# A gated linear attention and a feed-forward layer: scores by halves of 64 keys in two more units, with a new order of all work

## The chip, the cores and the metric

The kernel runs on one core of a Trainium2 chip. Its time is the time of one execution on the device in microseconds; the figure of a kernel is the median over runs. Three runs of the kernel before gave 575.72, 575.88 and 578.43, median 575.88 us.

## What is computed

For each of 4 batches and 8 heads, a state of 48 x 48 complex numbers is decayed by a complex factor per key row and step, and takes in the outer product of key and value; the output is the query times the real part of the state. The result goes through a feed-forward layer with the gate h * tanh(softplus(h)).

```python
mag = np.sqrt(a_re * a_re + a_im * a_im)
scale = np.minimum(mag, 0.999) / (mag + 1e-06)
a_re_n, a_im_n = a_re * scale, a_im * scale
for t in range(S):                        # S = 768, D = 48
    new_re = ar * S_re - ai * S_im        # ar, ai: step t of a_re_n, a_im_n
    new_im = ar * S_im + ai * S_re
    S_re, S_im = new_re + outer(k[t], v[t]), new_im
    y[t] = q[t] @ S_re
h = x @ w_in                              # x: y with heads side by side, 3072 x 384; w_in 384 x 2048
out = (h * np.tanh(softplus(h))) @ w_out  # w_out 2048 x 384
```

## The kernel before, in words

The 3072 tokens are cut into 12 units of 256 (three for each batch), a unit into two chunks a and b of 128 tokens. For a unit, `elementwise` turns decay factors into growth and angle per step, scales queries and keys by them and sends the result through DMAs ("relay": tiles X and QK into T, six for a chunk) into a layout with the 96 rows of one head below each other.

`attention` then does, for each chunk: transposes of the keys (`kn`, tile pkn), the scores keys x queries in two groups of four heads (`am`, tile pa), their masking by VectorE (`am_out`, tiles am or kept), the weighted sums of the values plus the old state times the queries (`y`, tile ypsum), and the new state (`pd`, `add`). The output moves by DMA (`x move`) into the input of the feed-forward layer `moe`. There each unit from 1 on has eight pairs p0 to p7 of 256 columns of the hidden layer. A pair has first-layer matmuls (`mm1`, tile ph, line 787), the gate (exp, square, ln and inv on ScalarE, cap and gate on VectorE, tile e and g), the split into a high and a low half (gh, gl) and second-layer matmuls (`mm2`, tile po, line 824). Unit 0 does it in blocks q0 to q3 for each chunk, without a split. The weights arrive as 64-bit words; VectorE and ScalarE turn them into floats in the first part of the run.

Scores exist in two forms, chosen by the unit's number against `HALF`. In one piece (line 637), a head is one matmul of 128 keys by 128 queries, and the mask is one VectorE instruction of 128 x 512 (line 652). By halves (line 644), the first 64 keys go with all 128 queries and the last 64 keys with the last 64 queries only, two heads side by side in the two column halves of the array. The mask is then three instructions (line 659, into one of two kept tiles whose unused corners are zeroed once), and the odd heads' weighted sums read values whose halves are swapped (`Vs`, loaded beside V).

No engine's order is left to a scheduler: each operation has a number by its place in the program text, and the table `ORDER` lists them as they are issued. A letter behind a number puts the operation on another engine than its first choice (V VectorE, A ScalarE, G GpSimd, T TensorE, S SyncE). Each engine works through its own part of that list in order, and SyncE's part is the queue of its DMAs: a DMA whose data isn't there yet holds all behind it. Eighty matmuls on a constant ("spins", line 886) fill TensorE at the start.

Of the kernel before, what the change touches and what calls it, by code (L numbers as in the profile page):

```python
# [25 lines left out]
DM, DF = H * D, 2048  # L26
P = 128
# [5 lines left out]
NCH = TU // C  # L33
# [13 lines left out]
HALF = 3  # L47
# [8 lines left out]
72 0 1 73 127 3 74 2 75 128 7V 5 8 76 10V 4 9 11 77 6 12 192 78 13 202 197 14 79 24V 80 27V 81 82 25 83 169V 15 19 28  # L56
26 132V 84 16 166V 85 133 22 17 86 167 23 87 31 170 88 32 135V 18 134 34 33 29 137 89 21 136 90 20 91 42 47 46G 45 92
35 48 30 49 93 43 36 44 194 50 193 53 52 94 139 39 95 54 195 96 55 97 40 51 98 37 196V 99 38 100 56A 60 207 101 62A
140 562 102 204 57 563 103 203V 104 199 105 41 200 106 61A 138 107 58 64 108 142 109 59 205 112 66 116 67A 68 113 118
65A 117 70 71A 114 206V 123 69 198 110 119 217 141 120 124 115V 121 201V 125 430 63 143 209 212 126 567 208V 210 144  # L60
122 146 186 211V 145 130 168 153 570V 147A 185 173 171 149 148 568 184 151 111 218V 187 174 155 154 571G 360A 129 175
150V 160 152 156 222 157 432 219 569 158 220 356 163 573 161 164 214 159 221V 273 172 189 357 215 188 213 272 191 162
176 216V 361A 190 358 177 359 227 274 165 363 178 575 275 365 367 276 364 223 224 282 366 572 181A 368 277 225 283 369
576 232 182 179 370 226V 278 292 131 180 229 237 284 279 293 376A 371 183 230 280 374 228 578 574 281 285 231V 372
375A 286 303 378 242 373 287 233V 386 234 388 362 583 302 235 387 382 389 390 288 236V 294 392 434 289 247 383 295 304
312 584 296 385 238 239 379 290 391 381A 384 393 297 380 291 240 442 743 305 243 395 377 244 577 241V 394 298 245 252
306 397 744 400 307 246V 398 446 299 401 257 248 579 322 396 399 308 402 249 403 448 405 580 313 749 404 250 406 323
314 581 251V 407 582 315 262 309 409 316 564 585 408 594A 317 565 300 593 586 324 253 254 301 436 410 431 318 411 263
255 412 258 325 264 414 326 256V 415 587A 417 265 450 267 418 413 332 266V 327 421 259 440 420 433 310 328 566 588 452
423 333 422 438 319 260 343 334 329 589 335 320 592 321 590 428V 595 435 336 311 591 596 426 424 330 337 429 597 603  # L70
342 602 598 338 331 425 344 604 427 268 269 601 339 463 750 747 345 609 270 346 462 607 752 474 261V 475 340 347 271V
341 606 751 416 437 348 476 349 350 351 599 605 444 612 608 477 464 419 456 478 610 454 439 753 757 487 354 613 600
441 755 465 479 352 466 355 611V 758 443 616 617 467 445 614 754G 615 621 619 353 480 618 623 468 759 622 481 486 469
760 447 756 498 488 761 624 458 499 765 470 500 489 490 628 936 511 471 762 472 626 944 501 473 625 491 620 629 627
449 745 631 492 764 630 510 493 451 502 935 941 482A 632 635 522 633 634 766 503 512 504 523 483 484 494A 746 636 453
513 505 455 942 495 485 496 497 514 524 525 515 767 506 763 459 516 526 517 507 768A 527 639 534 769 518 774 535 528
792 775A 529 508 509 641 776A 536 547 537 519 546 771 778 772 781 530A 520 531 642 779 773 637 638 780 640 785 787 788
521 532 533 644 786 791 538 643 539 548 549 540 541 793 655 457 943 460 946 656 550 542A 543 544 461 545 551 782 945G
645 646 777 552 770 553 947 948 783 957 554 668 796 958 797V 794 959 667 748 555 784 798 960 647 648 795 649 650 1127
799 961 949 657 658 950 669 800 556 651A 557 801 670 790 679 558 802 652 805 1133V 962 659 803 952 560 660 671 1128  # L80
661 807 808 806 662 653 940 951 680 953 804 789 809 672 810V 1134 954 811 692 681 682 812 815 816 813 1136 814 663A
1135 691 818 673 559 683 956 939 938 1138 674 820 955 664 684 965V 817 822 819V 654 665 666 937 967 693 561 685 694
704 968A 686 703 715 675A 676 677 826 964 678 969A 971 966 1137 974 1140 825 828 978 827 695 984 716 696 697 698 982
687A 688 728 963 1141 970 1149 705 706 689 699A 1150 700 823 707 708 981 690 701 702 821 717 727 718 1151 709 1139 979
# [12 lines left out]
1045 1513 1036 1046 1064 1053 1357 1047A 1054 1198 931V 1063 1514 1522 1055 1056 1356 1075 1065 1347 1057 933V 1199
1355 1048 1515 1066 1352 1200 1523 1037 1038 1049 1524 932 1343 1203 1204 1516 1058 1059 934 1076 1067 1201 1068 1069
1050 1077 1070 1087 1078 1079 1080 1081 1060 1517 1088 1518 1089 1520 1090 1061 1202 1082 1091 1205V 1519 1207 1092
1093 1071 1502 1099 1206 1100 1101 1062 1532A 1525 1526 1072 1529V 1102 1103 1208 1112 1360 1361 1111 1358 1359 1349  # L100
1083 1084 1094 1095 1113 1073 1362 1364 1363 1501 1365 1691 1114 1074 1210 1531 1697 1209 1104 1105 1366 1106 1371
1096 1369 1372 1700V 1115 1370 1116 1117 1698 1367 1085 1701 1222 1699 1702 1528 1118 1533G 1373 1535 1536 1368 1704
1086 1537 1530 1542 1534 1221 1211 1212 1223 1224 1107 1374 1527 1097 1098 1375 1108 1376V 1119A 1233 1213 1120 1538
1214 1703 1215 1225 1226 1234 1109 1216 1217 1873 1705 1227 1110 1121 1122 1123 1257 1228 1379 1229 1377 1706 1218
1235 1236 1237 1544 1380 1124 1541 1378 1230 1713 1238 1714 1715 1239 1240 1241 1874 1546 1258 1543 1245 1125 1126
1539 1246 1707 1247 1248 1545 1547 1386 1249 1250 1381 1382 1387 1384 1270 1540 1259 1260 1383V 1391 1390 1251 1252
1261 1262 1263 1219 1220 1231 1232 1879 1880 1716 1242 1264 1269 1385 1708 1709 1293 1253 1265 1271 1272 1710 1389
1281 1254 1504 1882 1881 1884 1273 1274 1275 1395 1396 1392 1397 1398 1276 1393 1294 1295 1243 1296 1244 1394 1883G
# [105 lines left out]
def tile_kernel(ctx, tc, q, k, v, vs, are, aim, are_t, aim_t, w_in, w_out, out):  # L214
# [900 lines left out]
```

## Time and profile before

| what | before |
|---|---|
| median of three runs | 575.88 us |
| the profiled execution, its own time | 579.47 us |
| its span, first to last instruction | 577.7 us |
| TensorE matmul busy | 567.0 us (98%) |
| VectorE busy | 482.4 us (83%) |
| ScalarE busy | 471.8 us (82%) |
| granted clock of TensorE | 0.998 |

The span is what the trace covers; the rest of the execution lies around it. An engine's busy share is an average over the run; how full it is in a stretch is a matter of the slices and of the table by stretches.

### The profile page before, as it was taken

To read this page: it belongs to the slowest core of one execution; us is meant where nothing else is said; L and a number is where in the kernel's file an instruction comes from. 1 tells how busy PE (TensorE), PEld (TensorE's weight loads), DVE (VectorE), ACT (ScalarE), POOL (GpSimd) and SP (SyncE) were. 2 spreads that over 40 slices of the span, in tenths; PEclk is the share of its full clock that TensorE was granted. 3 is DMA by queue.
4 is the path that set the end of the run, shared out by engine and by line. 5 is a ranking of instruction groups with operands and counts; after the bars stand their busy time and mean duration, and the time that the engine had idled before them with its cause. 6 is when DMAs were issued, how large, how long until landed. Compare 5 with 4: busy or idle time off the path is not lost.

```text
span 577.7 us, 13275 instructions
## 1 busy us (share of the span) xinstructions
PE 567.0 (98%) x5262; PEld 532.3 (92%) x5262; DVE 482.4 (83%) x899; ACT 471.8 (82%) x759; POOL 29.5 (5%) x59
## 2 busy tenths in 40 slices
PE   8999999999999999999999999999999999999996
PEld 4689788899999999999999999999999999999995
DVE  5999999999999999989979997998876867556453
ACT  7899999999999999888977688868967868456671
POOL 2010000110000010200002000300000000000000
PEclk9999999999999999999999999999999999999999
DMA  8688874521626345262244145072253260010100
GB/s 297 235 275 267 251 237 131 168 58 38 196 77 177 108 128 159 60 188 61 65 135 146 23 133 163 19 211 75 59 145 101 65 170 1 15 44 0 56 2 33
DMA packets 58469, 68.91 MB, mean 119 GB/s; under 512 B 4976, under 2 KB 51440, under 8 KB 58400
## 3 DMA queue, kind: packets, MB, share of 16 engines
q1 hardware_dynamic: 57616, 67.14, 39.5%
q8 instruction: 43, 0.70, 0.5%
q10 hardware_dynamic: 720, 0.66, 0.4%
q14 instruction: 26, 0.21, 0.1%
q0 software_dynamic: 64, 0.20, 0.1%
HBM read 39.52 MB, written 4.72 MB: 77 GB/s over the span
## 4 chain that ended last, share of the span: by engine, by line
PE 74%; ACT 12%; DVE 7%; DMA 3%; issue 2%; POOL 1%; SPq 0%; ACTq 0%; DVEq 0%; POOLq 0%
PE ph L787 30%; PE po L824 29%; PE ypsum L674 6%; PE pa L644 4%; ACT X L174 3%; PE pd L689 3%; ACT L172 2%; ACT e L174 2%; PE pkn L622 2%; DMA words<-w_out 1%; DMA words<-w_in 1%; DMA T<-QK 1%; ACT words L174 1%; ACT R L174 1%; DVE w L296 1%
## 5 line engine op out<-in xcount | busy, mean ns | idle before, releaser
L174 ACT ACTIVATE e<-e 128x512 f32<-128x512 f32 x192 | 119.1, 629 | 27.6 <-DVE e L856 25.4
L787 PE MATMUL ph<-xH,wh 128*128 128x256 f32 x462 | 133.3, 289 | 0.0
L787 PE MATMUL ph<-xL,wh 128*128 128x256 f32 x462 | 129.9, 281 | 0.0
L787 PE MATMUL ph<-xH,wl 128*128 128x256 f32 x462 | 129.8, 281 | 0.0
L824 PE MATMUL po<-wh,gh 128*128 128x384 f32 x308 | 105.0, 341 | 0.0
L824 PE MATMUL po<-wh,gl 128*128 128x384 f32 x308 | 103.5, 336 | 0.4 <-DVE gl L812 0.4
L824 PE MATMUL po<-wl,gh 128*128 128x384 f32 x308 | 103.6, 336 | 0.0
L787 PEld LDWEIGHTS ph<-xH,wh 128*128 128x128 f32 x462 | 87.0, 188 | 1.8 <-issue 0.7
L787 PEld LDWEIGHTS ph<-xL,wh 128*128 128x128 f32 x462 | 87.0, 188 | 0.3 <-DVE xL L758 0.3
L787 PEld LDWEIGHTS ph<-xH,wl 128*128 128x128 f32 x462 | 87.0, 188 | 0.0
L800 DVE SCALAR_TENSOR_TENSOR g<-e,ph 128x512 f32<-128x512 f32 x96 | 65.1, 682 | 22.9 <-ACT e L174 19.8
L174 ACT ACTIVATE e<-ph 128x512 f32<-128x512 f32 x96 | 56.6, 592 | 26.4 <-PE ph L787 21.9
L812 DVE TENSOR_TENSOR gl<-g,gh 128x512 fp32r<-128x512 f32 x88 | 63.7, 725 | 10.1 <-PE po L824 8.7
L174 ACT ACTIVATE e<-e,fifth 128x512 f32<-128x512 f32 x96 | 69.4, 723 | 1.9
L824 PEld LDWEIGHTS po<-wh,gl 128*128 128x128 f32 x308 | 57.9, 188 | 0.7 <-DVE gl L812 0.7
L824 PEld LDWEIGHTS po<-wh,gh 128*128 128x128 f32 x308 | 57.9, 188 | 0.6 <-issue 0.2
L824 PEld LDWEIGHTS po<-wl,gh 128*128 128x128 f32 x308 | 57.9, 188 | 0.0
L856 DVE TENSOR_SCALAR e<-e 128x512 f32<-128x512 f32 x96 | 42.5, 445 | 17.8 <-ACT e L174 17.5
L172 ACT ACT_TABLE_LOAD x36 | 46.2, 1283 | 0.6
L659 DVE TENSOR_TENSOR kept<-pa,cmask 64x128 f32<-64x128 f32 (+1 forms) x108 | 32.6, 329 | 13.4 <-PE pa L644 10.6
L674 PE MATMUL ypsum<-T,S 96*48 96x128 f32 x320 | 34.3, 275 | 0.0
L174 ACT ACTIVATE X<-X 128x768 f32<-128x768 f32 (+1 forms) x40 | 30.2, 764 | 0.2
(145 smaller groups left out, 1116.5 us busy)
## 6 DMA issues: line engine op xcount, KB each, us to landing
T<-QK SPq DMA_DIRECT2D x70, 129.0 KB, 2.8
T<-X SPq DMA_DIRECT2D x69, 129.0 KB, 2.6
words<-w_in SPq DMA_DIRECT2D x8, 768.0 KB, 6.4
words<-w_out SPq DMA_DIRECT2D x8, 768.0 KB, 6.5
QK<-k SPq DMA_DIRECT2D x12, 384.0 KB, 5.4
QK<-q SPq DMA_DIRECT2D x12, 384.0 KB, 5.6
V<-v SPq DMA_DIRECT2D x12, 384.0 KB, 4.3
R<-a_re SPq DMA_DIRECT2D x12, 384.0 KB, 4.2
```

Source lines behind the costliest of these rows:

```text
L172: self.nc.scalar.preload_act_table_set(need)
L174: return self.nc.scalar.activation(out, in_, func, **kw)
L622: e.transpose(d["pkn", g][:, i, :], T()[:, 4 * g + i, 1, :C], ident)
L644: e.matmul(d["pa", g][r0:r0 + C // 2, i, k0:], T()[:, 4 * g + i, 1, k0:k0 + C // 2], T()[:, 4 * g + i, 0, k0:C], start=True, stop=True)
L659: e.tensor_tensor(x[r, :, two, t], y[r, :, two, t], m[r, :, two, t], ALU.mult)
L674: e.matmul(ypsum[64 * par:64 * par + D, i, :], lhs, rhs, start=m == 0, stop=first or m == 1)
L689: e.matmul(d["pd", g][r, i, :], d["kn"][:, h, r], st["V"][:, c, h * D:(h + 1) * D], start=not held, stop=not held or i == 3)
L787: e.matmul(ph[k][:, slot(k, j, a), :], win(x, j, kt, a), st[y][:, kt, cols(k)], start=n == 0, stop=n + 1 == len(todo))
L800: e.scalar_tensor_tensor(g_[k], e_[k], 2.5, ph[k], ALU.subtract, ALU.mult)
L812: e.tensor_tensor(gs[k][1], g_[k], gs[k][0].bitcast(F32), ALU.subtract)
L824: e.matmul(po[t], x[:, slot(k, j, a), 0 if halved else t * P:C if halved else (t + 1) * P], wout(y, j, a), start=j == 0 and a == 0 and n == 0,
L856: op("V", f"{n} cap", lambda e, k=k: e.tensor_scalar_min(e_[k], e_[k], math.exp(20.0)))
```

## The change

`HALF` goes from 3 to 1: units 1 and 2 have their scores by halves as well, and take `Vs` from a tile of their own with one buffer. The table `ORDER` is another one, with two more entries (the two loads of Vs). The numbers of the operations shift with these, so a line of it is not to be read against the other table.

```diff
-HALF = 3
+HALF = 1
...
-72 0 1 73 127 3 74 2 75 128 7V 5 8 76 10V 4 9 11 77 6 12 192 78 13 202 197 14 79 24V 80 27V 81 82 25 83 169V 15 19 28
+0 7V 8 1 9 10V 12 3 11 2 13 24V 72 73 14 128 25 15 27V 136V 26 74 16 127 170V 75 76 167V 77 78 79 80 81 82 83 168 19
...
+    EARLY = (1, 2)
...
         if u >= HALF:
-            st.homes["Vs"] = lambda: swapped["Vs"][:, u % 2]
+            if u in EARLY:
+                st.homes["Vs"] = io, "Vs", 1, [P, NCH, DM // 2]
+            else:
+                st.homes["Vs"] = lambda: swapped["Vs"][:, u % 2]
             op("S", f"Vs{u} load", lambda e: e.dma_start(st["Vs"], vs[u]))
```

Between the two programs, the matmuls of scores change from 48 + 144 + 144 (whole, first half, second half) to 16 + 176 + 176. On VectorE 12 masks in one piece and 108 of the halves become 4 and 132, and the two zero fills come from GpSimd. ScalarE has 40 table loads where it had 36. SyncE issues all 144 relays, where ScalarE issued five.

VectorE around the masks of unit 1's first chunk, in the order before (line 652 is the mask in one piece, 292, 296 and 300 are steps of the weights, 856 is the cap of a gate):

```order
L800 SCALAR_TENSOR_TENSOR g<-e,ph 128x512
L856 TENSOR_SCALAR e<-e 128x512
L515 SCALAR_TENSOR_TENSOR X_464<-rmask,I 128x384
L292 TENSOR_SCALAR w<-words 128x768
L652 TENSOR_TENSOR am<-pa,cmask 128x512 x2
L296 SCALAR_TENSOR_TENSOR w<-words,w 128x768
L856 TENSOR_SCALAR e<-e 128x512
```

The same place now (the lines behind 336 have moved by one, those behind 403 by four: 663 is the masks of the halves, 738 a zero fill, 860 the cap):

```order
L804 SCALAR_TENSOR_TENSOR g<-e,ph 128x512
L738 MEMSET kept 128x512
L292 TENSOR_SCALAR w<-words 128x768
L663 TENSOR_TENSOR kept<-pa,cmask 128x4x64
L663 TENSOR_TENSOR kept<-pa,cmask 64x2x64 x2
L296 SCALAR_TENSOR_TENSOR w<-words,w 128x768
L860 TENSOR_SCALAR e<-e 128x512
L515 SCALAR_TENSOR_TENSOR I<-ncar,I 128x3
L663 TENSOR_TENSOR kept<-pa,cmask 128x4x64
L663 TENSOR_TENSOR kept<-pa,cmask 64x2x64 x2
```

Two instructions have become six, with a zero fill ahead of them and two other steps between the groups.

TensorE at the first chunk of unit 2, before: its last state matmuls (pd), and what follows, three steps of nine first-layer matmuls (ph), the first three of the 27 rows shown:

```order
L689 MATMUL pd<-V,kn 64x48
L689 MATMUL pd<-V,kn 33x48
L787 MATMUL ph<-xH,wh 128x256
L787 MATMUL ph<-xL,wh 128x256
L787 MATMUL ph<-xH,wl 128x256
```

The same place now:

```order
L693 MATMUL pd<-V,kn 64x48
L693 MATMUL pd<-V,kn 33x48
L648 MATMUL pa<-T 64x128 x2
L648 MATMUL pa<-T 64x64 x2
L648 MATMUL pa<-T 64x128 x2
L648 MATMUL pa<-T 64x64 x2
L648 MATMUL pa<-T 64x128 x2
L648 MATMUL pa<-T 64x64 x2
L648 MATMUL pa<-T 64x128 x2
L648 MATMUL pa<-T 64x64 x2
L791 MATMUL ph<-xH,wh 128x256
```

Both groups of the second chunk's scores (pa) stand directly behind the first chunk's state; two of the three first-layer steps now follow them, and the third stands further ahead, among the first chunk's scores.

SyncE's queue from the relays of unit 2 on, before (T<-X and T<-QK are relays, out_dram the stores of unit 0's output):

```order
L566 DMA T<-X 16x8x258 x3
L566 DMA T<-QK 16x8x258
L566 DMA T<-X 16x8x258
L393 DMA V<-v 128x768
L566 DMA T<-QK 16x8x258 x3
L566 DMA T<-X 16x8x258
L566 DMA T<-QK 16x8x258 x2
L566 DMA T<-X 16x8x258
L841 DMA out_dram<-o 128x384 x2
L381 DMA I<-a_im 128x768
```

And now, from the relays' sixth on:

```order
L570 DMA T<-X 16x8x258 x3
L382 DMA I<-a_im 128x768
L382 DMA R<-a_re 128x768
L570 DMA T<-X 16x8x258
L570 DMA T<-QK 16x8x258 x2
L408 DMA Vs<-vs 128x384
L845 DMA out_dram<-o 128x384
L570 DMA T<-X 16x8x258
L394 DMA V<-v 128x768
L570 DMA T<-QK 16x8x258
L845 DMA out_dram<-o 128x384
```

The first store of unit 0 and a load of V have come in front of the last two relays of unit 2's second chunk, and two loads of unit 4 in front of three more.

## Rows read from the trace of the kernel before

**Rows 1.** The page's slices: busy tenths in 40 equal slices.
```profile
PE   8999999999999999999999999999999999999996
DVE  5999999999999999989979997998876867556453
```

**Rows 2.** Table by stretches: length, then busy time and instructions of each engine.
```profile
50.00:130.00 80.00, 78.41 (x670) 66.36 (x669) 77.71 (x123) 76.60 (x124) 5.58 (x6) 1.00 0.62 183
130.00:250.00 120.00, 119.39 (x1201) 115.98 (x1202) 115.78 (x213) 113.43 (x179) 6.83 (x10) 1.00 0.43 120
250.00:550.00 300.00, 299.99 (x2871) 294.07 (x2868) 232.89 (x457) 225.68 (x365) 10.04 (x14) 1.00 0.31 88
```

**Rows 3.** TensorE's waits, all seven: total us, times, longest.
```profile
PE junk L886 <- POOL cmask L235: 1.8, 1, 1.8
PE psum L418 <- DVE X L492: 0.9, 1, 0.9
PE pkn L622 <- DVE w L292: 0.8, 1, 0.8
PE pd L689 <- DVE am L652: 0.5, 2, 0.3
PE po L824 <- DVE gl L812: 0.4, 1, 0.4
PE pa L644 <- DVE kept L659: 0.3, 1, 0.3
PE pkn L622 <- DMA T<-QK: 0.3, 1, 0.3
```

**Rows 4.** Timeline of TensorE around scores: start, duration, line, tiles, shapes, count.
```profile
116.73 1.06 PE L637 MATMUL pa<-T 96*128 96x128 f32 x8
117.54 0.36 PE L787 MATMUL ph<-xH,wh 128*128 128x256 f32 x1
...
151.46 1.56 PE L644 MATMUL pa<-T 96*64 96x128 f32 x32
152.95 0.44 PE L824 MATMUL po<-whl,gh 128*128 128x384 f32 x1
...
204.51 0.34 PE L824 MATMUL po<-wh,gl 128*128 128x384 f32 x1
204.68 0.34 PE L824 MATMUL po<-wl,gh 128*128 128x384 f32 x1
204.95 0.89 PE L644 MATMUL pa<-T 96*64 96x128 f32 x16
205.67 0.39 PE L674 MATMUL ypsum<-T,S 96*48 96x128 f32 x4
```

**Rows 5.** Groups of VectorE by shape: count, busy us, mean ns, idle before.
```profile
L659 DVE TENSOR_TENSOR kept<-pa,cmask 64x128 f32<-64x128 f32 x72 | 20.4, 283 | 0.8
L659 DVE TENSOR_TENSOR kept<-pa,cmask 128x256 f32<-128x256 f32 x36 | 15.1, 420 | 12.7 <-PE pa L644 10.6 <-PE ypsum L674 1.8
L652 DVE TENSOR_TENSOR am<-pa,cmask 128x512 f32<-128x512 f32 x12 | 8.0, 679 | 0.5 <-PE pa L637 0.5
L629 DVE COPY kn<-pkn 128x384 f32<-128x384 f32 x14 | 7.7, 549 | 0.7 <-PE pkn L622 0.7
L267 DVE MEMSET ypsum<- 32x512 f32 x1 | 0.5, 485 | 1.0 <-PEq L1057 1.0
```

**Rows 6.** Timeline: the low half of unit 2's fourth pair, and its first reader.
```profile
176.96 0.68 DVE L812 TENSOR_TENSOR gl<-g,gh 128x512 fp32r<-128x512 f32 x1
...
178.45 0.34 PE L824 MATMUL po<-wh,gh 128*128 128x384 f32 x1
```

**Rows 7.** Timeline around unit 2's second chunk; last, a V load's us to landing.
```profile
113.43 0.39 PE L787 MATMUL ph<-xH,wh 128*128 128x256 f32 x1
...
108.79 0.48 ACT L835 ACTIVATE o<-po 128x384 f32<-128x384 f32 x1
...
V<-v SPq DMA_DIRECT2D x12, 384.0 KB, 4.3
```

More of the change, by code (lines that the diff above doesn't have):

```diff
@@ L60 @@
[L60 to L84, printed above, removed]
@@ L150 @@
[L150 to L152 removed]
+0 7V 8 1 9 10V 12 3 11 2 13 24V 72 73 14 128 25 15 27V 136V 26 74 16 127 170V 75 76 167V 77 78 79 80 81 82 83 168 19
+22 28 31 17 193 133V 134 195 84 4 32 171 85 86 87 88 18 23 89 196 90 34 29 91 92 93 94 95 20 21 33 203 204V 46G 42 205
@@ new lines @@
+459 446 352 614 615V 490 620 621 605 765 481 489 482 618 611 612 627 570 354 623 619 622 625 491 492 628 448 626 483
+484 473 606 751 613 632 629 760 450 630 501 355 457 624 631 943 599 633 485A 474 769 486 452 356 502 946 493 503 504
+634 454 494 495 496 635 636 749 640 639 513 475 514 944 505 506 770 461 507 515 766 497A 456 645 768 476 516 508 750
+458 638 498 526 525 767 646 517 487 488 527 518 643 509 771 519 528 772A 644 510 538 537 520 462 529 637 641 642 780
+521 773 530 531 499 500 511 549 532 539 540 775 947G 776 522 778 550 533A 512 534 779A 782 783 785 784 463 774 777 541
@@ new lines @@
+1319 846 1322 854 996 1158 1157 995 1002 1162G 743 1009 1133 1010 744 1164 1005 874 1006V 1165 1166 1003 997 745 1159
+1171 847 848 1174 1324 746 855 873 1007 863 1012 864 865 1004V 1014 1008 1011 866 856 857 867 875 876 877 1321G 1013
+858 868 1333 878 879 1015 869A 1016 880 898 1169 870 897 885 1334 886 1017 1018 887 888 1170 1167 899 900 1325 1173
+889 901 1323 902 1326 1019 1172 1023V 903 910 1502 859 1176 890 891 1335 860 1020 1336 871 872 1180 1021 881 1501 882
+883 1025V 1022 1027V 1177 1024 1026 1327 904 892 893A 1028 905A 1315 884 1181V 1178 1179 1328 1337 1329 909 1338 911
@@ new lines @@
+1202 1517 1519 1065 1201 1079 1204 1080 1209V 1527 1210 1066 1067 1062 1068 1081 1082 1083 1359 1520 1205V 1069 1070
+1207 1208 1352 1351 1348 1090 1084 1206 1085 1354 1071 1072 1089 1702 1051 1052 1091 1092 1362 1316 1363 1357 1521
+1063 1693 1360 1361V 1358 1522 1535 1101 1073A 1074 1102 1103 1528 1364 1366 1367 1064 1093 1086 1094 1095 1113 1104
+1105 1106 1114 1096 1097 1107 1503 1075 1211 1365 1076 1087 1534A 1088 1115 1116 1117 1118 1119 1108 1531V 1504 1533
+1098 1120 1371 1372 1368 1530 1369 1537 1699 1540 1121 1539 1373 1529 1374 1532 1544 1545 1548 1700 1876 1377 1224
@@ new lines @@
+1701 1212 1546 1378V 1213 1704 1375 1109A 1214 1110 1536 1543 1376V 1215 1235 1223 1216 1217 1550 1099 1100 1547 1111
+1112 1541 1122 1123 1542 1379 1505 1381 1370 1225 1226 1227 1228 1124 1218 1506 1219 1706 1703 1549 1875 1538 1707
+1236 1248 1705 1380 1220 1229 1382 1708 1715 1247 1695 1716 1230 1384 1717 1231 1232 1718 1237 1125 1719 1388 1386
+1238 1127 1128 1383 1249 1250 1251 1385V 1387 1389 1709 1252 1221 1239 1394 1260 1259 1222 1698 1233 1710 1711 1391
+1240 1234 1551 1241 1253 1242 1272 1243A 1244 1261 1262 1881 1271 1126 1393 1395V 1254 1263 1245 1553 1283 1264 1712
@@ new lines @@
+1273 1274 1392 1397V 1246 1255A 1396 1399V 1400 1284 1275 1276 1398 1265 1266 1277 1278 1279 1552V 1296 1256 1280 1720
+1401 1554 1713 1557 1558 1555 1556 1295 1390 1285 1696 1267A 1257 1297 1298 1884 1286 1258 1287 1288 1289 1268 1882
+1290 1291 1562 1564 1565 1563 1566 1885 1883 1886 1299 1402 1403 1404 1269 1270 1300 1281 1282 1413 1887 1292 1697
+1569 1714 1722V 1725A 1301 1723 1302 1414 1303 1293 1570 1294 1304 1305 1888 1721 1897 1425 1567 1726A 1724 1728 1732
+1306 1307V 1308 1426 1735 1405 1406 1559 1571 1727 1415 1416 1572 1560 1889 1890 1892 1568 1407 1573 1574 1730 1578
@@ new lines @@
+1737 1408 1409 1561 1575 1417 1418 1738 1427 1419 1428 1420 1580 1309 1410 1576 1891 1740 1421A 1422 1898 1899 1461
+1733 1739 1893 1437 1577 1584 1583 1429 1462 1430 1431 1581 1736 1585 1463 1464 1579 1900A 1465 1438 1432 1411 1412
+1466 1467 1894 1449 1439 1450 2065 1423 1424 1895 1468 1586 1474 1433A 1434 1741 1734 1451 1435 1436 1452 1896 1440
+1310 1441 1442 1443 1587V 1453 1454 1455 1901 1904V 1444 1445 1446 1729 1731 2071V 1589 1590 1473 1475 1476 1456 1588
+1457 1458 1907A 1591 1592 1486 2072 1447 1448 1485 1459 1460 1477 1478 1479 1744 1742 1469 1470 1471 2066 1480 1481
@@ new lines @@
+1482 1908 1743V 1593 2074 2075 1605 1745V 1472 1902 1582 1594 2073 2076G 1487 1748 1909 1877 1878 1746 1903 1906 1910
+1905 1917 1595 1596 1488 2078 1912 1747 1749 2087 2088 1489 1490 1491 1606 1483 1484 1750 1753 1754 1597 1598 1492
+1493A 1755 1756 1757 1751 1752V 1760 1761 1607 1608 1599 1758 1759 1918 1600 1920 1618 1763 1913 2258 1919 1911 1930
+2089 1494 2090 1762 1609 1610 1611 1612 1931 1617 1619 1620 1764 1767 2077 1765 1495 1621 1768 1601A 1602 1922 1622
+1496 1629 1499V 1500 1497 1923 1641 1630 1642 1916 1498 1915 1613A 1614 1914 1623 2091 1773V 1624 2079 1880 2080 2082
@@ new lines @@
+1631 1632 2081 1603 1604 1615 1633 2083 2084 1643 1644 1634 1654 1653 1635 1636 1637 2092 1616 1766 1677 1625A 1645
+1771 1626 2085 1772 1655 1656 1926 1627 1628 1646 1647 1774 1648 1769 1649 2266V 1770 2257 2093 1921 1924 1925V 1927V
+2263 2264 1666 2267 1879 1678 1657 1658 1665 2086 2098A 1638 1639 1659 1640 2067 2100 1660 1679 2095V 1680 2099 2265
+2268 1650 1935 1936 1661 1667 1928 1937 1668 1938 1929 1681 1682 1683 1684 1669 1670 1671 2094 2068 1787 2097 2101
+1651 2104 1672 2102 1788 1662 1776 2096 2069 1775 1941 1939 1673A 2108 1652 2114 1800 2110 1663 1664 2113 1674 1675
@@ new lines @@
+1676 1789 1777 1778 1790 1942V 1940V 1779 1780 1781 1782 1799 1685A 1686 1687 1688 2269 2271 1943 1932 2107 1791 1792
+1783A 1784 1793 1794 1801 2103 1933 1944 2109 1934 1691V 1945 1952 2270 1946 1947 1953 1689V 1948 1949V 2111 1795A
+1796 1802 1803 1950 2272 1951 1804 2262 1805 2119 1812 2120 2273 1955 2279 2280 2281 2274 1956 2282 1785 1811 2112
+1806 1813 1814 1848 1807A 2283A 1815 2275 2276 1786 1797 1808 1692 2260 1836 1957 1816 1817 1818 1819 1835 1690 1847
+1798 1809 2117 1959 1960 2115 1958 1849 1850 1961 1962 2277 1824 2070 1963 1954 1964 1837 1823 2105 2118 2116V 2121
@@ new lines @@
+1820 1851 1852 1853 1854 2106 2128 2122 1825 1826 1827 2123 2124 2129 2125V 2126 2135 1828 1829 1810 1838 2278 1839
+2127 2131 2130 1830 1831 1821 1822 1840 1841 1842 2136 1832 1843A 1860 1859 1861 1833 2132 2284 2286 2287 1844 2339
+2133 2134V 2285 2259 2288 2289 1834 1845 1862 2137 2139 2138 2290A 1863 2292 2298 2295 2294 2144 2145 2142 1864 1855A
+1856 1865 2299 2301 1866 1867A 2140 1965 1966 2141V 2148 1967 1977 1846 1978 1979 1980 2143 2146 2001 1868 1857 1858
+1869 2002 1968 1969 1970 1971 2147 1981 2302 1982 1972 1973 1974 1870 1871 1983 1984 2300 2291 2293 2310 1990 2003
@@ new lines @@
+2004 2005 1989 2014 2013 2304 1873 2006 1985 1986 2311 2007 1975 1976 1991 1992 1993 2306 1872 2008 2026 1987 1874
+1994 1995 1996 1997 2015 2016 2017 2018 2019 2020 2303 1988 2149 2153V 2037 2296 2038 2154 2025 2340 2027 2150 2155V
+2308 1998 1999 2000 2009 2010 2028 2011 2341V 2029 2050 2156 2021 2039 2151 2022 2152 2040 2030 2031 2032 2049 2307
+2309 2012 2041 2169 2042 2033A 2034 2170 2023 2024 2297 2305 2043 2044 2045 2261 2046 2312 2319 2314 2313 2320 2315
+2051 2052 2317 2324 2318 2322 2323 2158 2035 2036 2321 2325 2316V 2327 2326 2171 2053 2054 2055 2056 2157 2159 2057
@@ L153 @@
+2416 2417 2395 2435 2406A 2384 2385 2396 2397 2436 2437 2407 2408 2409 2426 2427 2428 2429 2418A 2419 2420 2438 2430A
+2439 2431 2421 2432 2440 2441 2442 2443 2444 2446 2447 2433 2445
 """.split()]
```

106 lines of the change are left out of this document (35 added, 71 removed), and 3 rows, old and new, of the table ORDER.

## The prediction

> **What bounds the kernel now.** I read the page's slices first, then the table by stretches, then TensorE's list of waits, and then single places in the timeline.
>
> In the slices [rows 1] the matmul line stands at 9 from the second slice to the last but one, while VectorE falls to 8 and below from the middle on. The stretches say the same in microseconds [rows 2]. From 250 to 550 us TensorE is busy for 299.99 of 300 and VectorE for 232.89, so the last half is TensorE's alone and VectorE has 67 us to spare. From 50 to 130 both are nearly full: VectorE 77.71 of 80 (2.3 idle), TensorE 78.41. From 130 to 250 VectorE is idle for 4.2 of 120 and TensorE for 0.6. So in the first 250 us TensorE's next matmul often waits for what VectorE has just made, and every wait there is added to the end, because nothing later can give it back. All TensorE waits that the profile names come to 5.0 us under seven causes; the longest is 1.8, in front of the first spin matmul, and the other six share 3.2 [rows 3]. The change can therefore earn little more than that, and can lose more.
>
> **The change part by part.**
>
> *Scores by halves in units 1 and 2.* Eight groups of four heads change form. A group in one piece holds TensorE for 0.81 us: it starts at 116.73 and the next matmul at 117.54 [rows 4]. A group by halves starts at 204.95 and the next matmul at 205.67, 0.72 us; ahead of it stand 0.27 us from the matmul at 204.68, where the step before was 0.17, so 0.10 more, 0.82 in all. Two groups behind each other take from 151.46 to 152.95, 1.49 us and with the same 0.10 ahead 1.59, against 1.62 in one piece. Four of the eight groups stand alone in the new order and four in two pairs: nothing for the singles, 2 x 0.03 for the pairs. Ends: 8 x (0.81 - 0.745) = 0.5 us gained with no change-over seen, 8 x 0.01 = 0.1 lost with all of them alone. I take 0.1 gained.
>
> The Trainium skill speaks against small column tiles here (TensorEngine Tiling (Array Packing), Tiling Modes): a change of tiling mode drains the engine. At its worst, by that rule, each of the twelve change-overs of four singles and two pairs would cost one matmul's 0.28 us, 3.4 us in all. Rows 4 hold such change-overs and show 0.10 us at entry, so the trace sides with the small cost.
>
> The weighted sums of the odd heads now read the swapped values: the same count of the same shape. The two loads for that (each as long as those of unit 3) have a buffer of their own; Vs1 stands ahead of the first relays, among the first loads, and Vs2 needs unit 1's weighted sums done, which stand on TensorE well ahead of unit 2's scores, so neither keeps the queue waiting.
>
> *VectorE.* A mask of one piece is one instruction of 679 ns; by halves it is three, 420 + 2 x 283 = 986 ns [rows 5]. That is 0.31 more for each of eight groups, 2.5 us. The two zero fills of the masked tiles move from GpSimd to VectorE; a fill as wide as these 512 columns took 485 ns there, so 1.0 us. Off VectorE, before the fourth pair of unit 2, go two copies of key rows (549 each) and one conversion of a weight word, counted alike, 1.65 us; the remaining small moves cancel (I count them as nothing: four come and three go, none longer than the pairs' cap). Sum ahead of that pair's low half: 2.5 + 1.0 - 1.65 = 1.85 us later. That low half ended at 176.96 + 0.68 = 177.64, and the first matmul that reads it began at 178.45 [rows 6]: 0.81 us to spare. If VectorE gives nothing back, TensorE waits 1.85 - 0.81 = 1.0 there, and the following pairs share that wait. If VectorE's idle time (2.3 in 50:130 and part of 4.2 in 130:250) swallows it, nothing. Ends 0 and 1.0; between them no row is nearer, and I take the middle, 0.5.
>
> *The knot at the second chunk of unit 2.* In the new order TensorE comes to these scores sooner: of the 27 first-layer matmuls that ran between 113.43 and 116.73 [rows 4, 7], 18 stand behind them now, 18 x 0.12 (3.30 / 27) = 2.2 us, so they are wanted at about 114.5. SyncE's queue moves the other way: the relays that feed them all stood ahead of unit 0's stores; now two of the six stand behind the first store, which waits for ScalarE's copy of that output half, and between these two stands a load of V. That copy ended at 108.79 + 0.48 = 109.27 [rows 7]; the order puts about as much ScalarE work ahead of it (I count 0.7 us less, so 108.6, an estimate). Then store, relay, V load and relay are issued at about 0.35, 0.6, 0.6 and 0.6 each: V starts near 109.6, and with 4.3 us to landing [rows 7] it is there at 113.9, the last relay just behind it at 114.2. That is 0.3 before it is wanted. I take 0.2 of wait, with ends 0 and 1.
>
> *The rest of the order.* ScalarE gets four more table loads, all in the stretch where it has idle time (225.68 of 300 busy in 250:550 [rows 2]) or shortly ahead of it, so nothing. In the head the loads of unit 2 and V1 move ahead of K0 and V0; K0 landed well before its use, and 38 spins still stand in front of the first transposes, so up to 1 us of delay there is covered by spins. At the end twelve second-layer steps follow the last first-layer one, where ten did, so the last chain has no less cover, and the tail stays.
>
> **Sum.** Against the profiled execution, whose own time is 579.47 (span 577.7): -0.1 + 0.5 + 0.2 = +0.6, 580.1. The median of the runs, 575.88, lies 3.6 below that execution, and the prediction is for such a median: 576.5 us.
>
> **Rivals.**
>
> *Faster: the new order closes the waits.* For it: each of the six waits behind the first spin is short and at another place, and the new order puts more matmuls ahead of the one that waited 0.4 us for a low half. Gain at most 3.2 for all of them and 0.5 from the halves: 575.9 - 3.7 = 572.2. Against it: VectorE and ScalarE have 2 to 3% idle up to 130 us and get more work, not less.
>
> *Slower: SyncE's queue holds the relays of unit 2.* The place is the store in front of the last two relays. ScalarE's copy stands behind nine instructions from pair 0's exponential on, among them that pair's square, which needs VectorE's cap first. Up to 0.3 us of delay costs nothing; beyond, each microsecond is one for the end. Were the copy as late as the other half's copy is moved (its place is some 10 us of ScalarE work later in the new order), say half of that, 5 us, the wait would be 4.7 and the time 575.9 + 0.4 + 4.7 = 581.0; at 3 us late, 579.0. Against it: ScalarE's prefix is no longer than before.
>
> *VectorE gives nothing back, anywhere.* The list has masks that TensorE waited for already, by 0.3 to 0.5 us [rows 3]; at such a place the 1.85 us count whole in place of my 0.5: 575.9 - 0.1 + 1.85 + 0.2 = 577.9, still inside the half per cent.
>
> *The drain of the tiling mode*, by the page named above: 575.9 + 3.4 - 0.1 = 579.2.
>
> **How the numbers follow.** A measurement of this kernel can tell 0.5%, 2.9 us, from no change: below 573.0 is faster, above 578.8 slower. Chances: forecast 0.51, waits closed 0.22, relays held 0.17, nothing given back 0.07, drain 0.03. The forecast's own range is 574 to 578.5, and I leave 0.02 of it on each side. Faster is then 0.21 (some closed waits gain less than 2.9) plus 0.02, 0.23; slower 0.16 + 0.03 + 0.02 = 0.21; the same 0.56. The range takes in the faster rival's end and most of the slower one: 572.0 to 580.5.
>
> **What would show it.** Right: TensorE's list of waits after grows by less than 2 us, with VectorE's low halves of units 2 and 3 as its causes; the masks by halves of units 1 and 2 take 0.93 to 1.0 us a group; 250:550 stays full. The relay term is wrong if the scores of unit 2's second chunk wait for a T transfer for over 1 us, and right with no such row. The forecast fails if TensorE's idle time before 250 us falls by 3 us, if it rises by 3, or if the stretch from 250 on is no longer dense, which I have taken as given from the old order.

## The result, and the profile after

Six runs of the changed kernel gave 581.97 to 586.21 us, median 583.60; six of the kernel before on the same chip 575.72 to 578.60, median 576.76. The ratio is 1.0098, with a 95% interval of 1.0073 to 1.0123: about 1% slower, 5.7 us by the ratio, and outside the range that was forecast. Below, a ratio is always to the kernel before as it ran beside that kernel, since its own median moved between 576.8 and 578.8 from one series to the next; it can differ from the quotient of two medians, by 0.2% here (583.60 / 576.76 is 1.0119, inside the interval). 0.1% is 0.58 us.

The profiled execution took 581.97 us (span 580.3, granted clock 1.000); it is the fastest of the six, and the profiled one of before (579.47) lies above its six, so the two are compared by their last matmuls and not by their times. The last matmul ends at 576.73 us where before it ended at 572.34, so TensorE is 4.4 us later. Of these, 2.4 are idle time; the other 2.0 stand as busy time (569.0 where it was 567.0), which the rows do not divide: a matmul's end is an estimate of the profiler's. The slices, to lay beside [rows 1]:

```profile
PE   8999999999999999999999999999999999999997
DVE  5999999999999998988888898989888865645643
```

The table by stretches, columns as in [rows 2]:

```profile
50.00:130.00 80.00, 77.05 (x726) 64.52 (x726) 79.00 (x134) 76.33 (x123) 5.88 (x4) 1.00 0.60 175
130.00:250.00 120.00, 117.94 (x1170) 114.24 (x1169) 114.82 (x213) 108.98 (x173) 7.81 (x8) 1.00 0.39 110
250.00:550.00 300.00, 299.55 (x2870) 292.35 (x2868) 239.32 (x469) 230.30 (x370) 3.12 (x11) 1.00 0.32 90
```

TensorE is idle for 2.95 us in the first stretch (1.59 before) and for 2.06 in the second (0.61), while VectorE has 1.00 idle in the first where it had 2.29 (in the second it has 5.18 idle where it had 4.22). From 250 to 550 TensorE is idle for only 0.45. Its list of waits, to lay beside [rows 3]:

```profile
PE junk L890 <- POOL cmask L235: 1.8, 1, 1.8
PE ph L791 <- DVE g L804: 1.3, 2, 1.0
PE pkn L626 <- DVE kept L663: 1.2, 1, 1.2
PE pa L648 <- DVE kn L633: 0.9, 1, 0.9
PE po L828 <- DVE gl L816: 0.6, 1, 0.6
PE pd L710 <- DVE kept L663: 0.4, 1, 0.4
PE ypsum L678 <- DVE am L656: 0.3, 1, 0.3
PE pa L648 <- DMA T<-X: 0.3, 1, 0.3
PE pa L648 <- DVE kept L663: 0.3, 1, 0.3
PE pkn L626 <- issue: 0.2, 1, 0.2
```

Seven causes and 5.0 us have become ten and 7.3. Seven of the ten are VectorE's, and three single waits of about 1 us stand out: a first-layer matmul on a gate (g), transposes on a mask (kept), scores on a copy of keys (kn). No wait is on a relay (T) for more than 0.3, and none is on ScalarE. The masks cost what was counted [rows 5]; these are the groups by shape:

```profile
L663 DVE TENSOR_TENSOR kept<-pa,cmask 64x128 f32<-64x128 f32 x88 | 24.9, 283 | 0.9
L663 DVE TENSOR_TENSOR kept<-pa,cmask 128x256 f32<-128x256 f32 x44 | 18.4, 418 | 3.2 <-PE pa L648 2.5 <-PE ypsum L678 0.4
L656 DVE TENSOR_TENSOR am<-pa,cmask 128x512 f32<-128x512 f32 x4 | 2.6, 682 | 0.0
L738 DVE MEMSET kept<- 128x512 f32 x2 | 1.0, 485 | 0.1
```

At the place on which the prediction had measured VectorE's lateness [rows 6], and at the second chunk of unit 2 [rows 4, 7], the timeline shows next to none:

```profile
114.22 1.83 PE L648 MATMUL pa<-T 96*64 96x128 f32 x31
115.98 0.39 PE L791 MATMUL ph<-xH,wh 128*128 128x256 f32 x1
...
178.94 0.68 DVE L816 TENSOR_TENSOR gl<-g,gh 128x512 fp32r<-128x512 f32 x1
...
179.83 0.33 PE L828 MATMUL po<-wh,gh 128*128 128x384 f32 x1
180.00 0.34 PE L828 MATMUL po<-wh,gl 128*128 128x384 f32 x1
```

The low half ends at 179.62. The matmul at 179.83 is the counterpart of the one in [rows 6], but it takes the high half (gh); the first that takes the low half (gl) starts at 180.00, 0.38 later, and does not wait. The scores of the second chunk start as soon as TensorE comes to them; they take 1.8 us in place of the 1.49 in [rows 4], since the weight load of their second group waits 0.23 for VectorE's addition to the state.

Halves standing alone take longer on TensorE than the prediction had it:

```profile
107.17 0.28 PE L791 MATMUL ph<-xH,wl 128*128 128x256 f32 x1
107.38 0.89 PE L648 MATMUL pa<-T 96*64 96x128 f32 x16
108.20 0.39 PE L791 MATMUL ph<-xH,wh 128*128 128x256 f32 x1
```

The group begins 0.21 behind the matmul ahead of it, where the step between first-layer matmuls is 0.12, and the matmul behind it begins 0.82 later: 0.91 in all, against 0.81 in one piece.

What stands ahead of the 1 us waits is seen in the timeline when GpSimd's row is read with VectorE's (860 is the cap of a gate, 715 the fade of a state, 483 the "size" step of units 4 and 6):

```profile
122.36 1.78 DVE L860 TENSOR_SCALAR e<-e 128x512 f32<-128x512 f32 x1
...
122.20 1.66 POOL L483 TENSOR_TENSOR X<-X 128x768 f32<-128x768 f32 x1 [15.38 <-ACT X L174]
...
125.78 0.38 PE L791 MATMUL ph<-xH,wh 128*128 128x256 f32 x1 [1.04 <-DVE g L804]
...
204.03 1.91 DVE L715 TENSOR_TENSOR S<-S,T 96x384 f32<-96x384 f32 x1
205.87 0.91 DVE L663 TENSOR_TENSOR kept<-pa,cmask 128x256 f32<-128x256 f32 x3
...
202.56 2.97 POOL L483 TENSOR_TENSOR X<-X 128x768 f32<-128x768 f32 x1 [0.55 <-DVE kept L663]
...
206.92 0.52 PE L626 MATMUL pkn<-identity,T 96*128 96x96 f32 x4 [1.19 <-DVE kept L663]
```

A cap takes 0.42 us elsewhere and a fade 0.55; here they take 1.78 and 1.91, and each ends 0.3 to 0.4 us behind GpSimd's instruction (123.86 and 205.53). The VectorE work queued behind them is late, and TensorE waits. The third wait (0.9, on kn) follows a cap beside unit 3's slope step (484) on GpSimd; from that cap to the copy of keys VectorE has no idle time:

```profile
105.47 1.62 DVE L860 TENSOR_SCALAR e<-e 128x512 f32<-128x512 f32 x1
...
102.70 4.06 POOL L484 TENSOR_TENSOR I<-I,X 128x768 f32<-128x768 f32 x1 [36.15 <-ACT X L174]
...
110.41 0.89 PE L648 MATMUL pa<-T 96*64 96x128 f32 x16 [0.88 <-DVE kn L633]
```

A fourth place, at 361.70 beside unit 10's slope step, has no wait behind it. The trace of before has such places too; which of all this costs what is a matter for runs.

### The profile page after: what moved, and what is told of

It is laid out like the page before. It is cut to its first block, busy times and chain, and to the rows that moved or that the text cites. A ratio compares the mean times of both kernels' runs of the same rounds, so it can differ in the third digit from the quotient of the medians.

```text
span 580.3 us, 13450 instructions
## 1 busy us (share of the span) xinstructions
PE 569.0 (98%) x5326; PEld 532.7 (92%) x5326; DVE 488.4 (84%) x917; ACT 477.3 (82%) x768; POOL 24.2 (4%) x52
## 4 chain that ended last, share of the span: by engine, by line
PE 66%; DVE 12%; ACT 11%; DMA 5%; issue 3%; SPq 2%; DVEq 0%; ACTq 0%
PE po L828 28%; PE ph L791 26%; PE ypsum L678 4%; PE pa L648 4%; ACT e L174 4%; PE pd L693 2%; ACT L172 2%; ACT X L174 2%; DVE kept L663 2%; DMA QK<-k 2%; PE pkn L626 1%; DVE g L804 1%; SPq L382 1%; DMA T<-X 1%; DVE wl L323 1%
## 5 line engine op out<-in xcount | busy, mean ns | idle before, releaser
L816 DVE TENSOR_TENSOR gl<-g,gh 128x512 fp32r<-128x512 f32 x88 | 60.3, 687 | 15.7 <-PE po L828 7.4
L663 DVE TENSOR_TENSOR kept<-pa,cmask 128x256 f32<-128x256 f32 x132 | 39.7, 328 | 4.1 <-PE pa L648 2.5
L648 PE MATMUL pa<-T 96*64 96x64 f32 (+1 forms) x704 | 37.8, 251 | 1.8 <-DVE kn L633 0.9
L648 PEld LDWEIGHTS pa<-T 96*64 96x64 f32 x704 | 33.5, 136 | 6.4 <-issue 2.2
```

Of the source, the lines that this page charges most:

```text
L648: e.matmul(d["pa", g][r0:r0 + C // 2, i, k0:], T()[:, 4 * g + i, 1, k0:k0 + C // 2], T()[:, 4 * g + i, 0, k0:C], start=True, stop=True)
L663: e.tensor_tensor(x[r, :, two, t], y[r, :, two, t], m[r, :, two, t], ALU.mult)
L816: e.tensor_tensor(gs[k][1], g_[k], gs[k][0].bitcast(F32), ALU.subtract)
```

## Experiments

Theory F: VectorE's extra work for the forms is the loss. Theory O: the new order's places are. The first four runs set them against each other. A kernel's order is shown by its numbers in the table; an entry without a letter runs on the operation's first engine, here VectorE for size and slope steps, GpSimd for fills.

**Forms alone.** Old order with the new forms:

```diff
-HALF = 3
+HALF = 1
+    Vs1 load behind V1 load, Vs2 load behind V2 load, both fills on VectorE
```

> Old order with only the forms changed: scores of units 1 and 2 by halves, the two Vs loads behind the loads of V1 and V2, the two zero fills on VectorE. Theory F (VectorE's work for the halves, 2.5 us of masks and 1.0 of fills, in a stretch where TensorE waits for it): 579 to 583 us, most of the 6.8 us that separate the medians 576.8 and 583.6. Theory O (the new order stands worse between 100 and 240 us, whatever the form): 576 to 578. Recorded prediction's own terms without the order: 576.8 - 0.1 + 0.5 to 1.85, 577.2 to 578.5.

Median 582.26, ratio 1.0078 (1.0052 to 1.0104). As theory F says, the forms alone cost 0.8%, more than the prediction's terms.

**Order alone.** New order with the old forms:

```diff
-HALF = 1
+HALF = 3
-132 570 387V 388V
+    (no Vs1, Vs2; both fills on GpSimd behind unit 2's sums)
```

> New order with the old forms: units 1 and 2 in one piece, no Vs1 and Vs2 loads, the zero fills back on GpSimd behind unit 2's weighted sums. Theory F: 575 to 578 us, no change to before, since VectorE has 3.5 us less to do than in the changed kernel. Theory O: 581 to 584, as the changed kernel, since the places stay as they are. If both take part, between: 579 to 581.

Median 580.66, ratio 1.0054 (1.0035 to 1.0073): between the theories, so the order costs as well. The two single costs add up to 1.3% where the change as a whole cost 1.0. The intervals leave room for a plain sum, so whether the new order carries the forms better than the old one isn't shown.

**Less and more VectorE work at the same places.**

```diff
-                        e.tensor_tensor(x[r, :, two, t], y[r, :, two, t], m[r, :, two, t], ALU.mult)
+                        if u not in EARLY or r == slice(0, P):
+                            e.tensor_tensor(x[r, :, two, t], y[r, :, two, t], m[r, :, two, t], ALU.mult)
```

> The changed kernel without the two small masks (64 x 128 elements each) of each of the eight groups in units 1 and 2: the scores of a chunk's early queries with its early keys are left out there, so that VectorE has 16 instructions of 0.28 us, 4.5 us, less to do. Theory F: 579 to 580.5 us (3 to 4.5 less than 583.6). Theory O, VectorE not what TensorE waits for in the main: 582.5 to 584.

```diff
                         e.tensor_tensor(x[r, :, two, t], y[r, :, two, t], m[r, :, two, t], ALU.mult)
+                        if u in EARLY and r != slice(0, P):
+                            e.tensor_tensor(x[r, :, two, t], y[r, :, two, t], m[r, :, two, t], ALU.mult)
```

> The changed kernel with the same two small masks done twice in units 1 and 2: 16 instructions of 0.28 us, 4.5 us more VectorE work at the same places. Theory F: 586.5 to 588 us (3 to 4.5 more). Theory O: 583.5 to 585. A slope of one third to two thirds would say that VectorE's idle time (2 to 4 us in the first 240) takes part of each us.

With fewer: median 580.22, ratio 1.0046 (1.0024 to 1.0069). With more: 588.76, 1.0196 (1.0163 to 1.0229). Against 1.0098, 4.5 us less VectorE work give back 0.52%, 3.0 us, and 4.5 us more cost 0.98%, 5.7 us: 0.67 and 1.25 us for each us of VectorE. Each of the two rates has an interval of 0.4 to 0.5 either way, so they are not told apart; from the fewer masks to the more it is 1.50%, 8.7 us for 9.1, 0.96 for each us. Theory F held for the first and fell short of the second. TensorE's list with more masks starts with the state's first matmuls behind a mask:

```profile
PE pd L712 <- DVE kept L665: 1.9, 3, 1.1
PE junk L892 <- POOL cmask L235: 1.8, 1, 1.8
PE pkn L626 <- DVE kept L663: 1.2, 1, 1.2
```

VectorE's work at these places is paid nearly in full.

**Where in the order.** Old forms, one half of the run in each order; at the cut, unit 7's arctan (1512), the two orders have done the same operations but for three. Shown is the new order with the old one behind it; the other run has them the other way round.

```diff
 ... 1342A 1185 1512
+1511 1337 1194 1692 ...
```

> Old forms (no change in units 1 and 2), the new order up to unit 7's arctan (some 240 us) and the old order for everything behind it; at that point the two orders have done the same operations but for three. Theory L (the new order loses in its later part, where TensorE's waits rose by 2.9 us behind 240 us in the trace of the new order with old forms, and gains 1.6 ahead of it): 0.9 to 1.8 us faster than before, 576.3 to 577.2 against 578.1. Theory E (the loss of 2.6 us that the new order showed with old forms lies in the first 240 us): 580 to 581. Nothing to tell apart (the 2.6 come from the end of the run, behind the last matmul): 578.

> The other half: old forms, the old order up to the same point and the new order behind it. Theory L: 2.5 to 3.5 us slower than before, 580.6 to 581.6. Theory E: 578, as before. If the two parts add up, the change of this run and of the one with the parts the other way round give the 2.6 us of the new order with old forms.

New then old: median 579.94, ratio 1.0026 (1.0011 to 1.0042). Old then new: 579.06, 1.0018 (1.0000 to 1.0036). Neither theory L nor theory E held as stated: the parts add up within their intervals (0.44% against 0.54). Which half has the larger share can't be told (0.26 and 0.18%), and the second's is at the edge of none.

**GpSimd's steps on VectorE.** The collisions seen in the timeline, tested in both kernels:

```diff
-758G 947G 1321G 2076G
+758 947 1321 2076
```

> The changed kernel with four elementwise steps of 128 x 768 (u3 slope, u4 size, u6 size, u10 slope) on VectorE in place of GpSimd: 4 x 0.95 us more work for VectorE. In the changed kernel's trace VectorE instructions of 0.42 to 0.56 us took 1.6 to 2.0 while these ran, 1.2 to 1.6 us lost each time, and TensorE's three longest waits (0.94, 1.20, 1.07) follow such places. Theory C (these collisions are a part of the loss): 0.5 to 2 us faster than the changed kernel, 581.5 to 583 against 583.6. Rival, the work itself counts: 3 x 0.95 ahead of 250 us at the measured 0.67 to 1.25 us for each us of VectorE, 1.9 to 3.6 us slower than it, 585.5 to 587.

```diff
-754G 945G 1319G 1883G 2074G
+754 945 1319 1883 2074
```

> The same move in the kernel before (u3 slope, u4 size, u6 size, u9 size, u10 slope from GpSimd to VectorE). In its trace five VectorE instructions lose 1.0 to 1.4 us each to these steps. Theory C as a general matter: 0 to 1.5 us faster than before, 576.5 to 578. Rival, the work itself counts: 2 to 3.5 us slower, 580 to 581.5.

In the changed kernel: median 580.59, ratio 1.0040 (1.0020 to 1.0059), 0.58% or 3.3 us better than 1.0098, although VectorE has 3.8 us more of its own to do (four steps of 0.95). In the kernel before: 578.27, ratio 1.0004 (0.9989 to 1.0019), nothing, with 0.9 to 1.4 us lost at each of five places and five steps of 0.95 in exchange. At the two places of the changed kernel, the timeline now has:

```profile
122.69 0.42 DVE L860 TENSOR_SCALAR e<-e 128x512 f32<-128x512 f32 x1
...
204.29 0.55 DVE L715 TENSOR_TENSOR S<-S,T 96x384 f32<-96x384 f32 x1
204.76 0.92 DVE L663 TENSOR_TENSOR kept<-pa,cmask 128x256 f32<-128x256 f32 x3
```

and TensorE's waits on gate, mask and kn at these places are gone. But the same trace has new ones, of the move itself and of relays:

```profile
102.65 0.96 DVE L484 TENSOR_TENSOR I<-I,X 128x768 f32<-128x768 f32 x1 [0.81 <-ACT X L174]
...
104.26 1.56 PE L828 MATMUL po<-w,g 128*128 128x384 f32 x4 [1.19 <-DVE g L804]
...
PE pkn L626 <- DMA T<-QK: 1.5, 1, 1.5
...
PE pkn L626 <- DMA T<-X: 1.2, 1, 1.2
```

VectorE now stands idle for ScalarE in front of unit 3's slope step, and the gate behind that step is late for TensorE. This wait of 1.2 to 1.3 us is in all four traces of the new order with the steps moved, so the gain of 0.58% is net of it. No other edit that leaves the work whole takes as much of the loss away, and the kernel before gains nothing by it.

**SyncE's queue.** In traces of the new order a relay of u0a, u4a or u9a (the first chunk of units 0, 4 and 9) was late in some and on time in others: TensorE waits for one by at most 0.3 us in the changed kernel's trace, by 1.5 with the steps moved, by 1.9 with fewer masks and by 2.4 in the run new then old. The mend, alone and with the steps moved:

```diff
-131 ... 132 ... (loads of V1, Vs1 ahead of unit 0's relays)
+    131 132 behind unit 0's relays
-1311 ... 984, 2258 1919 1911
+    seven relays of unit 4 ahead of 1311; 1919 1911 2258
```

> The changed kernel with SyncE's queue mended at three places: the loads of V1 and Vs1 behind the first chunk pair's relays, the seven relays of unit 4 ahead of the loads of R6, I6 and V4, two relays of u9a ahead of the load of I11. Everything else stays, GpSimd's steps too. Theory D (TensorE's first use of u0a, u4a and u9a follows the last relay's landing by 0.14 to 0.6 us in the new order, and waited up to 2.5 us there in single runs): ratio to before 1.0045 to 1.0075, 1.5 to 3 us less than the changed kernel's 1.0098. Rival (relays are hidden but in single runs): 1.009 to 1.010.

> Both mends in the changed kernel: the queue as in the run with relays first, and the four steps moved from GpSimd to VectorE (which alone brought the ratio from 1.0098 to 1.0040). If collisions and relays are the whole loss besides the masks: 0.999 to 1.0015, some 577.5 to 579 us against 578.4. If the relays are hidden: 1.004.

Relays first: median 583.66, ratio 1.0096 (1.0068 to 1.0124). With both: 581.35, 1.0053 (1.0024 to 1.0082). Theory D's forecast fell: unit 4's last relay, issued at 185.88 and landing 2.4 us later, was there 2.6 us ahead of its use at 191.01, and the time stayed. The list of the first of these shows what came in place of late relays:

```profile
PE pkn L626 <- DVE kept L663: 1.2, 1, 1.2
PE ph L791 <- DMA x<-y: 1.1, 1, 1.1
PE ph L791 <- DVE g L804: 1.1, 1, 1.1
PE po L828 <- DVE gl L816: 1.0, 1, 1.0
PE pa L648 <- DVE kn L633: 0.9, 1, 0.9
```

The waits on VectorE are as before the mend, and there is a new one, of 1.1 us on the moves of unit 0's output (x<-y; 1.5 with both mends); the loads of V1 and Vs1 now stand ahead of these moves in the queue. So the mend traded one wait for another: what late relays cost in the executions that have them stays open.

**Order and forms without these steps on GpSimd.** The same edit of letters on the two single changes:

> Old forms, new order, the four steps on VectorE. The new order with old forms stood at 1.0054. If its loss came by the collisions with GpSimd, 0.999 to 1.001 here; if by the relays or the places of VectorE's work, still 1.004 to 1.006. The difference to the changed kernel with this move (1.0040) is the price of the forms in the new order without collisions: 0 to 0.004.

> New forms in the old order, the five steps on VectorE (the move that changed nothing in the kernel before: 1.0004). The forms in the old order stood at 1.0078. If a part of that came by the collisions, 1.003 to 1.006; if it is VectorE's 3.5 us of masks and fills at 0.67 to 1.25 us each and nothing else, 1.004 to 1.0078 and the move changes nothing.

Order alone: median 579.29, ratio 1.0024 (1.0005 to 1.0043), against 1.0054 with the steps on GpSimd, between the two forecasts; the difference just exceeds its interval. Forms alone: 582.31, 1.0080 (1.0057 to 1.0103), against 1.0078. So moving the steps pays in the new order, and not in the old one with either form. But the forms in the old order had a collision of their own, beside unit 2's size step, which was still on GpSimd:

```profile
36.88 1.74 DVE L288 TENSOR_SCALAR words<-words 128x768 int32<-128x768 uint32 x1 [0.16 <-DMA words<-w_out]
...
36.60 1.55 POOL L483 TENSOR_TENSOR X<-X 128x768 f32<-128x768 f32 x1 [20.67 <-ACT X L174]
...
39.26 0.57 PE L710 MATMUL pd<-S,identity 96*97 96x192 f32 x2 [1.33 <-DVE am L656]
```

In the kernel before the same weight step went ahead of GpSimd's, which took longer instead:

```profile
36.59 1.99 POOL L479 TENSOR_TENSOR X<-X 128x768 f32<-128x768 f32 x1 [20.66 <-ACT X L174]
...
36.62 0.55 DVE L288 TENSOR_SCALAR words<-words 128x768 int32<-128x768 uint32 x1
```

**What the forms' price consists of.** Old order, new forms, unit 2's size step on VectorE too, and then the same with fewer masks and the fills on GpSimd:

```diff
-575G
+575
```

> New forms in the old order, as in the run with five steps on VectorE (ratio 1.0080), and unit 2's size step on VectorE as well. In both traces of the forms in the old order a weight step of 0.55 us took 1.74 to 1.94 at 36.7 us beside that size step on GpSimd, the mask behind it was late and TensorE waited 1.3 us; in the trace of before it took 0.55. If this collision belongs to the forms' price: 1.003 to 1.006. If it is chance of a single run, or the 0.95 us more for VectorE weigh as much: 1.007 to 1.0095.

> The same kernel without the two small masks of each group in units 1 and 2 (scores of a chunk's early queries with its early keys are left out there) and with the zero fills on GpSimd: VectorE has 8 x 0.26 = 2.1 us less for these masks than in the kernel before, not 3.5 more. If VectorE is the whole price of the forms: 0.997 to 1.001. If TensorE's halves with their change-overs, or the two Vs loads, cost in their own right: 1.003 to 1.006.

The first: median 582.44, ratio 1.0062 (1.0039 to 1.0086), within its interval of 1.0080, so what that one collision costs stays open. The second: 578.33, 0.9991 (0.9974 to 1.0008). With 5.5 us less VectorE work (16 x 0.283 of masks, 2 x 0.485 of fills) the price of the forms is gone: 0.71%, 4.1 us, 0.75 for each us (0.4 to 1.1 by the intervals). The traces show the places. The first has these waits; in the second the first two are gone, and of the third 0.30 us are left (at 111.96):

```profile
72.12 1.60 PE L791 MATMUL ph<-x,w 128*128 128x128 f32 x12 [1.38 <-DVE g L804]
...
90.35 1.60 PE L791 MATMUL ph<-x,w 128*128 128x128 f32 x12 [0.63 <-DVE g L804]
...
115.28 0.42 PE L678 MATMUL ypsum<-kept,V 128*48 128x128 f32 x2 [0.72 <-DVE kept L663]
```

TensorE's halves and the loads of Vs are in both. By the time alone they could still cost some 2 us, since VectorE has 2.1 us less for these masks than in the kernel before.

**The fills.** The changed kernel, with the four steps on VectorE and the fills on GpSimd:

```diff
-387V 388V 758G 947G 1321G 2076G
+387 388 758 947 1321 2076
```

> The changed kernel with the four steps on VectorE (1.0040 alone) and the two zero fills back on GpSimd, 1.0 us less for VectorE ahead of 60 us. At 0.67 to 1.25 us for each us of VectorE: 1.002 to 1.003. If these early fills are hidden: 1.004.

Median 580.30, ratio 1.0036 (1.0016 to 1.0055), against 1.0040: nearer to hidden fills, but the intervals hold both forecasts. Its profiled execution (577.59, the fastest of its twelve) has 0.8 us of waits on relays where that of the run with the fills on VectorE (582.33) has 3.2, and its last matmul ends at 572.33, as in the kernel before (572.34), where the other's ends at 575.14. Single executions show no price, but late relays may well be part of what remains. No kernel tried is faster than the one before by more than its interval.

## Why the prediction was wrong

**The step that failed is VectorE's.** Its extra work was counted rightly: 418 + 2 x 283 ns for a group by halves, two fills of 485. Its price was not. The prediction measured the room at one reader of a low half (0.81 us), let idle time swallow half of the excess and took 0.5, with 1.0 at most. (It also took the wrong matmul: the one at 178.45 reads the high half, and the first on the low half began at 178.62, so the room was 0.98.) That reader did not wait. The work was paid at others that had no room: gates, masks and key copies whose results TensorE wanted at once. The runs give 0.67 to 1.25 us of time for each us of VectorE in units 1 and 2, 0.96 over both, and 0.78% (4.5 us) for the forms in the old order; at these rates VectorE's 3.5 us are 2.3 to 4.4 of them. The rival "gives nothing back, anywhere" had the right mechanism; its 1.85 us were still too few, as they left out the collisions and all else that the order costs.

**What the sum did not have: GpSimd beside VectorE.** The terms counted the busy time of VectorE's instructions by their usual durations. In the changed kernel four of them lose 1.2 to 1.6 us each to GpSimd's size and slope steps, and taking these steps away brought 0.58%. The kernel before loses as much at five such places (5.9 us against 5.5), and there the same move brought nothing (1.0004). Behind two of its five TensorE waits for 0.4 and 0.3 us (gl and kept in [rows 3], at 129.74 and 208.58), where the changed kernel waits for 0.9, 1.0 and 1.2 behind three of four. No run prices the collisions apart from the moved steps; as far as these go, it is the place in the order that makes a collision dear. And "the rest of the order", taken at 0, was not 0: with the old forms the order cost 0.54%, and 0.24% without the steps on GpSimd. In the new order without them the forms cost little more: 1.0040 against 1.0024, a difference inside the intervals, so their price there isn't settled.

**The other terms.** Halves on TensorE, 0.1 gained: by the same way of adding it is about 0.3 lost, 0.10 for each of four singles less 0.03 for each of two pairs. The prediction saw the change-over into the halves (0.10) but took its 0.72 from a place where weighted sums follow; in front of a first-layer matmul it is 0.82. A drain of 0.28 at each change-over is excluded: the rows at 107.38 show about 0.1 on either side. The relays of unit 2, 0.2: no wait there. SyncE's queue: the mend at three places brought nothing, but with the new wait on x<-y it doesn't clear the relays. ScalarE's four more table loads, at nothing: no wait on ScalarE stands in TensorE's list. The stretch from 250 us on, taken as dense: 0.45 us idle up to 550. This holds in the trace, though the run with the new order in its later part alone stood at 1.0018, at the edge of what can be told from none. "Waits close" was the wrong way round: some old waits went, and longer ones came. Of the signs that the prediction named, the list of waits gave the warning (2.3 us more, where less than 2 was to be right, and not by low halves but by gates, masks and keys); idle time before 250 us rose by 1.9, short of the 3 that were to mean failure.

What remains of the loss in the changed kernel with the steps moved, 0.40%, has in its trace the wait of 1.2 us that the moved slope step makes, waits on relays that differ from one execution to the next, and small waits on masks. The runs do not divide it further.

## What to carry to other kernels

Where one engine is full and another waits for it at many places, price extra work at nearly its whole length, not by the room at the one place that can be seen; two runs, with less and with more of the work at its own places, give the rate. Read GpSimd's rows beside VectorE's: an instruction that takes three times its usual length is a wait that no list of waits shows. And a new order is to be judged by what stands behind such places, since taking them away brought nothing in one order and 0.58% in the other.

## What the runs showed of the hardware

VectorE's blocked instructions show as long, not as idle: 1.62 to 2.02 us for steps of 0.42 to 0.55 in the changed kernel and in the runs of the forms in the old order, each ending 0.3 to 0.5 us behind GpSimd's. GpSimd is held as well: its slope step took 4.06 us at 102.70, with several VectorE steps of usual length beside it, and 1.83 at 361.61. Which engine is held can hang on hundredths of a us: a weight step that began 0.03 us behind GpSimd's size step took 0.55 us and GpSimd's 1.99, and one that began 0.07 us behind it (in the first run of the forms in the old order) took 1.94 and GpSimd's 1.55. These are two pairs of rows, and the profile's times for GpSimd are rough. The Trainium skill states a rule for this (SBUF — State Buffer, Who interferes with whom): the two engines share a pair of ports as an exclusive lock, and "issue order, not op shape, decides who blocks". The traces agree in that now one and now the other of the two is held; a start that the profile shows first is not always the winner, as the row at 36.59 has it.

The stretch behind the last matmul has two lengths: 5.35 us in the profiled execution of before and 3.55 in that of the changed kernel (spans 577.69 and 580.28), with the same work in it. In the seventeen traces of this case it is 3.5 to 3.7 us in four and 4.9 to 5.7 in the others. In two profiled executions whose times are compared, that alone can be 1.8 us.
